# Float32 loads through staging tiles on the hardware DMA queue, q and k by half sequence, reciprocals spread from ScalarE's queue

## The chip, the cores and the metric

The kernel runs on one core of a Trainium2 chip. The metric is the device time of one execution in microseconds (us), as the median of three runs. The engines of the core are named as in the profile: PE (TensorE, with PEld for its weight loads), DVE (VectorE), ACT (ScalarE), POOL (GpSimd) and SP (SyncE, which only issues DMAs here). A name with q behind it (SPq, POOLq) is the sequencer of that engine.

## The reference

Two stages follow each other. First attention over 4 batches, 8 heads, 768 positions and 64 features a head; heads 0, 2 and 6 see all earlier positions, the other five see the first 4 positions (the sinks) and a window of the last 64. Then a feed-forward layer over the 3072 rows, with a gate.

```python
scores = scale * np.matmul(q, k.transpose(0, 1, 3, 2))
stream_keep = causal & (is_sink | in_win)          # heads that are not "retrieval"
scores = np.where(mask[None], scores, -1e9)
a = np.exp(scores - np.max(scores, axis=-1, keepdims=True))
a = a / (np.sum(a, axis=-1, keepdims=True) + 1e-09)
x = np.matmul(a, v)                                # (4, 8, 768, 64) -> (3072, 512)
h = x @ w_in                                       # 512 -> 2048
g = h * (1.0 / (1.0 + np.exp(-beta * h)))
out = g @ w_out                                    # 2048 -> 512
```

All inputs are float32: q, k and v have 6.3 MB each, the two weights 4.2 MB each.

## The kernel before

The work is cut into 8 units: a batch and one half of its 384-query halves (u = 0 or 1). A unit goes through four steps. *pieces_a*: transposes of q and k on PE, scores on PE, their exponential on ACT, masks on DVE, and `sums`, the row sums by PE with a DVE reciprocal `rec`. *pieces_b*: `pv`, the product with v on PE, scaled on DVE into `xT`. *mm1*: 16 steps of four 128x384 matmuls into `h`, each with a tanh on ACT (`t`) and a product on DVE (`gT`). *mm2*: 16 steps of three 128x512 matmuls into `o`, copied by ACT (`osb`) and stored by SP.

The heads go in four pairs. A window head uses a gathered copy of its keys (`KX`, 12 blocks of 128 columns: 4 sinks and 124 positions) and the same of its values (`vs`); the other heads use `KT` and `vr`.

The reciprocals lie one query to a column, with one row to a head, and have to be spread over 64 partitions each. They go through DRAM: three DMAs write `rec` to `rd`, two DMAs read `rd` back 64-fold into `R`. `xT` needs `R`. All five are issued by SP.

All loads are issued by POOL, as DMAs that turn float32 into bfloat16 on the way. q and k come for a whole batch (four DMAs for each pair of heads), v with a POOL copy of the sink rows for each window head. POOL also makes the identity matrix for the transposes and the masks, behind the loads of batch 0 in its program.

The outer loop runs n from 0 to 8. In step n, mm1 of unit n and mm2 of unit n-1 go in 16 steps, and between them the side work: `pv` of unit n+1, then *pieces_a* of unit n+2, so `sums` of unit n+2 is its last piece. Loads of the next batch are issued ahead of a step. Each engine works its instructions off in their order, which a scheduler fixes when the program is built; tiles have a fixed number of buffers in their pool (for example `ps_m` and `ps_h` two, `inp` four).

Of the kernel before, what the change touches and what calls it, by code (L numbers as in the profile page):

```python
# [42 lines left out]
def kernel(  # L43
# [18 lines left out]
    NP = len(PAIRS)  # L62
    W = 64
# [9 lines left out]
    inp = pool("inp", 4)  # L73
    qkp = pool("qkp", 2)
# [14 lines left out]
    def load_pair(b, pi):  # L89
        d = {}  # L90
# [7 lines left out]
        return q2, k2  # L98

    def load_v(b):  # L100
        vr = vp.tile([128, 3, T, D], BF16, name="vr")
        vs = vp.tile([128, 5, NBLK, D], BF16, name="vs")
        sk = vp.tile([SINK, 5, D], BF16, name="sk")
        vpos = {}
        nr = ns = 0
        for pi, pr in enumerate(PAIRS):
            for h in pr:
                if RETR[h]:
                    nc.gpsimd.dma_start(out=vr[:, nr], in_=v[b, h].rearrange("(t p) d -> p t d", p=128))  # L109
                    vpos[h] = nr  # L110
                    nr += 1
                else:
                    vb = v[b, h]
                    nc.gpsimd.dma_start(out=vs[:, ns, 0, :], in_=vb[0:128, :])  # L114
                    nc.gpsimd.dma_start(  # L115
                        out=vs[:, ns, 1:NBLK, :],
                        in_=bass.AP(vb.tensor, vb.offset + (FIRST - W - SINK) * D,
                                    [[D, 128], [STEP * D, NBLK - 1], [1, D]]),
                    )
                    nc.gpsimd.dma_start(out=sk[:, ns, :], in_=vb[0:SINK, :])  # L120
                    nc.gpsimd.tensor_copy(  # L121
                        out=vs[0:SINK, ns, 1:NBLK, :],
                        in_=sk[:, ns, :].unsqueeze(1).to_broadcast([SINK, NBLK - 1, D]),
                    )
                    vpos[h] = ns
                    ns += 1
        return vr, vs, vpos

    qk_in = {}
    v_in = {}  # L130
    for pi in range(NP):
        qk_in[0, pi] = load_pair(0, pi)
    v_in[0] = load_v(0)


# [51 lines left out]
    FS = d_ff // 4  # L187
    for s in range(4):
        for pi, (ha, hb) in enumerate(PAIRS):
            for i, h in enumerate((ha, hb)):  # L190
                nc.gpsimd.dma_start(  # L191
                    out=w_in_sb[i * D:(i + 1) * D, pi, s * FS:(s + 1) * FS],
                    in_=moe_w_in[h * D:(h + 1) * D, s * FS:(s + 1) * FS],
                )
    for s in range(4):
        nc.gpsimd.dma_start(
            out=w_out_sb[:, s * 4:(s + 1) * 4, :],
            in_=moe_w_out[s * 512:(s + 1) * 512, :].rearrange("(fo fi) d -> fi fo d", fi=128),
        )


    qkT = {}

    def transpose_pair(b, pi):
        q2, k2 = qk_in.pop((b, pi))
        ha, hb = PAIRS[pi]
        qt_ps = ps_m.tile([128, T, 128], BF16, name="misc")
        for t in range(T):
            nc.tensor.transpose(qt_ps[:, t, :], q2[:, t, :, :].rearrange("p a d -> p (a d)"), ident)  # L209
        QT = qkp.tile([128, 128, T], BF16, name=f"QT{pi}")  # L210
        nc.vector.tensor_copy(out=QT, in_=qt_ps.rearrange("d t p -> d p t"))
        kt_ps = ps_m.tile([128, T, 128], BF16, name="misc")
        for t in range(T):
            nc.tensor.transpose(kt_ps[:, t, :], k2[:, t, :, :].rearrange("p a d -> p (a d)"), ident)  # L214
        KT = KX = None
        flat = kt_ps.rearrange("d t p -> d (t p)")
        if pi == 0:
            KT = qkp.tile([128, 128, T], BF16, name="KT0")
            nc.vector.tensor_copy(out=KT, in_=kt_ps.rearrange("d t p -> d p t"))
            KT = KT.rearrange("d p t -> d (p t)")  # L220
        else:
            lo = 0
            if pi == 1:
                KT = qkp.tile([128, S], BF16, name="KT1")
                nc.vector.tensor_copy(out=KT[0:64, :], in_=flat[0:64, :])
                lo = 64
            KX = qkp.tile([128, NBLK, 128], BF16, name=f"KX{pi}")
            src = flat[lo:128, :]
            nc.vector.tensor_copy(out=KX[lo:128, 0, :], in_=src[:, 0:128])
            nc.vector.tensor_copy(  # L230
                out=KX[lo:128, 1:NBLK, SINK:128],
                in_=_view(src, FIRST - W, [[STEP, NBLK - 1], [1, 124]]),
            )
# [203 lines left out]
    for f in pieces_l(2):  # L437
        f()
# [50 lines left out]
```

## Time and profile before

| | |
|---|---|
| runs | 312.59, 315.05, 316.58 us, median 315.05 us |
| profiled execution | 314.46 us, its span 312.8 us |
| mean granted clock of TensorE | 0.976 |
| busy | PE 255.1, DVE 147.1, ACT 135.9, POOL 141.7 us |
| DMA moved | 28.66 MB |

Busy time is the union of an engine's instructions; the ends of matmuls are modelled, so a busy PE may still be held up. Instructions that issue DMAs are not busy time in the page's first part. Where one engine waits for another, the profile names the releaser that came last.

### The profile page before, as it was taken

The numbers are of one execution on the slowest core, as the hardware profiler recorded it, in microseconds if no ns is written. First come the engines' busy times: TensorE is split into PE (matmuls) and PEld (weight loads), VectorE is DVE, ScalarE is ACT, GpSimd is POOL, SyncE is SP. The second block draws the span as 40 slices with busy tenths as digits, with TensorE's granted clock in tenths as the row PEclk, the third lists the DMA queues.
The fourth block names the chain that finished last, engine by engine and source line by source line (L and its number), as shares of the span: only waits on it lengthen the run. The fifth ranks groups of instructions, "written<-read, shape, count | busy, mean of one in ns | idle before, by whom it ended". The sixth has DMA issues, their size and how long they took to land.

```text
span 312.8 us, 5541 instructions
## 1 busy us (share of the span) xinstructions
PE 255.1 (82%) x2196; PEld 132.4 (42%) x2196; DVE 147.1 (47%) x309; ACT 135.9 (43%) x217; POOL 141.7 (45%) x208
## 2 busy tenths in 40 slices
PE   0000477659699979999999799999999999999994
PEld 0000353325355433555554345555544455555541
DVE  0000583143489644629773445397736554444410
ACT  1000134513344765534544386355547843455521
POOL 8999899728689967869994100000000000000000
PEclk9999999999979995999999799999999999999999
DMA  9998589999999999989999300500050024000011
GB/s 65 123 102 56 53 108 127 180 217 137 179 80 67 108 202 140 83 134 112 133 111 189 61 34 4 136 34 36 3 135 36 34 67 106 36 35 34 36 67 67
DMA packets 106539, 28.66 MB, mean 92 GB/s; under 512 B 95057, under 2 KB 103441, under 8 KB 106513
## 3 DMA queue, kind: packets, MB, share of 16 engines
q0 software_dynamic: 96256, 15.62, 67.2%
q1 hardware_dynamic: 10256, 12.69, 14.4%
q8 instruction: 17, 0.28, 0.4%
q14 instruction: 10, 0.07, 0.1%
HBM read 37.52 MB, written 6.39 MB: 140 GB/s over the span
## 4 chain that ended last, share of the span: by engine, by line
PE 58%; DMA 21%; POOL 9%; DVE 6%; SPq 2%; issue 2%; ACT 1%; DVEq 0%; POOLq 0%; ACTq 0%
PE o L389 22%; PE h L378 22%; DMA R<-rd 13%; PE sp L291 5%; DMA rd<-rec 4%; PE misc L369 4%; DMA sk<-in_v_dram 3%; PE misc L332 3%; PE misc L214 2%; DVE rec L338 2%; PE misc L209 1%; POOL w_in_sb L191 1%; SPq L345 1%; POOL vs L115 1%; SPq L341 1%
## 5 line engine op out<-in xcount | busy, mean ns | idle before, releaser
L381 ACT ACTIVATE t<-h,beta_h 128x384 f32<-128x384 f32 x128 | 74.3, 582 | 91.0 <-PE h L378 87.9
L378 PE MATMUL h<-xT,w_in_sb 128*128 128x384 bf16 x512 | 110.0, 335 | 0.1
L389 PE MATMUL o<-w_out_sb,gT 128*128 128x512 bf16 x384 | 105.9, 384 | 0.0
L382 DVE SCALAR_TENSOR_TENSOR gT<-t,h 128x384 bf16<-128x384 f32 x128 | 70.4, 552 | 71.4 <-ACT t L381 70.2
L378 PEld LDWEIGHTS <-w_in_sb 128*128 128x128 bf16 x512 | 45.6, 99 | 40.3 <-issue 7.9
L389 PEld LDWEIGHTS <-gT 128*128 128x128 bf16 x384 | 37.0, 98 | 32.6 <-issue 2.4
L209 PE MATMUL misc<-ident,q_99 128*128 128x128 bf16 x6 | 0.8, 303 | 32.6 <-DMA vs<-in_v_dram 32.6
L370 DVE TENSOR_TENSOR xT<-misc,R 128x384 bf16<-128x384 f32 x32 | 16.8, 550 | 13.1 <-DMA R<-rd 10.9
L115 POOL DMA_DIRECT2D vs<-in_v_dram x20 | 21.8, 1092 | 2.1 <-DMA q_642<-in_q_dram 1.7
L121 POOL COPY vs<-sk 4x704 bf16<-4x704 bf16 x20 | 15.2, 762 | 15.7 <-DMA sk<-in_v_dram 8.6
L393 ACT ACTIVATE osb<-o 128x512 f32<-128x512 f32 x24 | 14.3, 594 | 9.1 <-PE o L389 8.6
L293 ACT ACTIVATE es_0_255<-sp 128x768 bf16<-128x768 f32 x2 | 1.6, 811 | 37.9 <-PE sp L291 37.9
L191 POOL DMA_DIRECT2D w_in_sb<-in_moe_w_in_dram x32 | 16.7, 561 | 0.7 <-DMA w_in_sb<-in_moe_w_in_dram 0.7
L369 PEld LDWEIGHTS <-vs 128*64 128x64 bf16 x260 | 9.2, 122 | 15.7 <-issue 15.6
L209 PEld LDWEIGHTS <-q_99 128*128 128x128 bf16 x6 | 0.6, 133 | 32.5 <-issue 32.5
L139 DVE CAST ident<-ident_f 128x128 bf16<-128x128 f32 x1 | 0.2, 227 | 28.2 <-POOL ident_f masks.py:199 28.2
L332 PEld LDWEIGHTS <-esel 128*32 128x32 bf16 x372 | 9.8, 101 | 7.3 <-issue 6.7
L114 POOL DMA_DIRECT2D vs<-in_v_dram x20 | 11.7, 583 | 1.1 <-DMA k_637<-in_k_dram 0.9
L109 POOL DMA_DIRECT2D vr<-in_v_dram x12 | 10.0, 853 | 3.4 <-DMA k_1454<-in_k_dram 2.8
L120 POOL DMA_DIRECT2D sk<-in_v_dram x20 | 10.4, 524 | 0.0
L369 PEld LDWEIGHTS <-vr 128*64 128x64 bf16 x108 | 7.1, 115 | 7.6 <-issue 5.8
L338 DVE RECIPROCAL rec<-misc 96x128 f32<-96x128 f32 x8 | 7.6, 953 | 4.4 <-PE misc L332 4.4
(376 smaller groups left out, 295.8 us busy)
## 6 DMA issues: line engine op xcount, KB each, us to landing
R<-rd SPq DMA_DIRECT2D x16, 384.0 KB
out_dram<-osb SPq DMA_DIRECT2D x24, 256.0 KB
vs<-in_v_dram POOLq DMA_DIRECT2D x20, 176.0 KB, 4.2
w_in_sb<-in_moe_w_in_dram POOLq DMA_DIRECT2D x32, 64.0 KB, 3.7
w_out_sb<-in_moe_w_out_dram POOLq DMA_DIRECT2D x4, 512.0 KB, 12.6
vr<-in_v_dram POOLq DMA_DIRECT2D x12, 96.0 KB, 4.6
rd<-rec SPq DMA_DIRECT2D x24, 4.0 KB
vs<-in_v_dram POOLq DMA_DIRECT2D x20, 16.0 KB, 2.8
```

The lines of the kernel that those rows point to most:

```text
L115: nc.gpsimd.dma_start(out=vs[:, ns, 1:NBLK, :], in_=bass.AP(vb.tensor, vb.offset + (FIRST - W - SINK) * D, [[D, 128], [STEP * D, NBLK - 1] ...
L121: nc.gpsimd.tensor_copy(out=vs[0:SINK, ns, 1:NBLK, :], in_=sk[:, ns, :].unsqueeze(1).to_broadcast([SINK, NBLK - 1, D]),)
L191: nc.gpsimd.dma_start(out=w_in_sb[i * D:(i + 1) * D, pi, s * FS:(s + 1) * FS], in_=moe_w_in[h * D:(h + 1) * D, s * FS:(s + 1) * FS],)
L291: nc.tensor.matmul(o[j][0], o[j][1], o[j][2], start=True, stop=True)
L332: nc.tensor.matmul(sm[32 * j:32 * j + 32, 0:128], esel[:, hpos[h], :, :].rearrange("p a b -> p (a b)"), e, start=(done[j] == 0), stop=(don ...
L369: nc.tensor.matmul(a, l, r, start=st, stop=sp)
L370: nc.vector.tensor_mul(x.xT[:, pi, :], o[:, 0:NQ], x.R[:, pi, :])
L378: nc.tensor.matmul(h[:, 0:NQ], w_in_sb[:, pi, fi * 128:(fi + 1) * 128], x.xT[:, pi, :], start=(pi == 0), stop=(pi == NP - 1))
L381: nc.scalar.activation(out=t, in_=h[:, 0:NQ], func=AF.Tanh, scale=beta_h[:, fi:fi + 1])
L382: nc.vector.scalar_tensor_tensor(out=x.gT[:, fi, :], in0=t, scalar=1.0, in1=h[:, 0:NQ], op0=ADD, op1=MULT)
L389: nc.tensor.matmul(x.o, x.gT[:, fi, ns * 128:(ns + 1) * 128], w_out_sb[:, fi, :], start=(fi == 0), stop=(fi == FO - 1))
L393: nc.scalar.activation(out=osb, in_=x.o, func=AF.Copy, scale=0.5)
```

## The change

All input loads leave POOL. They become float32 DMAs issued by SP into staging tiles, and a cast by an engine follows: k on DVE, q on DVE for batch 0 and on POOL later, v and its sink rows on POOL, the weights on POOL except for two quarters of `w_in` on DVE. q and k are loaded, cast and transposed by half sequence, one DMA for each tensor, pair and half, in runs of 768 bytes; v is loaded by half too, in runs of 256 bytes. Staging tiles have 4 buffers (q, k), 5 (v) or 2 (weights), so a load waits for the cast of the tile that had its buffer. `KX` is kept by half, copied from the transposed keys in SBUF. The order of the outer loop changes: in step n the side work is *pieces_a* of unit n+2 without `sums`, then `pv` of unit n+1, then `sums`; the loads for later units are spread over the 16 steps. The five DMAs that spread the reciprocals are issued by ACT.

```diff
-    inp = pool("inp", 4)
-    qkp = pool("qkp", 2)
+    stg = pool("stg", 2)
+    inp = pool("inp", 2)
+    qkp = pool("qkp", 1)
...
+    def load_pair(b, u, pi):
         ha, hb = PAIRS[pi]
-        q2 = inp.tile([128, T, 2, D], BF16, name="q2")
-        k2 = inp.tile([128, T, 2, D], BF16, name="k2")
-        kfmt = "(p t) d -> p t d" if pi == 0 else "(t p) d -> p t d"
-        for i, h in enumerate((ha, hb)):
-            nc.gpsimd.dma_start(out=q2[:, :, i, :], in_=q[b, h].rearrange("(p t) d -> p t d", t=T))
-            nc.gpsimd.dma_start(out=k2[:, :, i, :], in_=k[b, h].rearrange(kfmt, t=T))
+        for nm, src, eng in (("q2", q, nc.vector if n_first(b, u) else nc.gpsimd), ("k2", k, nc.vector)):
+            f = stg.tile([128, 2, TU, D], F32, name=nm + "f", bufs=4)
+            nc.sync.dma_start(
+                out=f,
+                in_=bass.AP(src.tensor, src.offset + ((b * H + ha) * S + u * NQ) * D,
+                            [[TU * D, 128], [(hb - ha) * S * D, 2], [1, TU * D]]),
+            )
+            c = inp.tile([128, TU, 2, D], BF16, name=nm)
+            cast(eng, c.rearrange("p t a d -> p a t d"), f)
...
+    def load_v(b, h, half):
+        f = stg.tile([128, NBLK // 2, D], F32, name="vf", bufs=5)
...
+        nc.sync.dma_start(
+            out=f[:, w0 - n0:n1 - n0, :],
+            in_=bass.AP(vb.tensor, vb.offset + (FIRST - W - SINK + STEP * (w0 - 1)) * D,
+                        [[D, 128], [STEP * D, n1 - w0], [1, D]]),
+        )
+        cast(nc.gpsimd, vs[:, i, n0:n1, :], f)
+        cast(nc.gpsimd, vs[0:SINK, i, w0:n1, :], sk[:, h, :].unsqueeze(1).to_broadcast([SINK, n1 - w0, D]))
...
+    def load_w_in(s):
+        f = stg.tile([128, 4, FS], F32, name="wf")
...
+        cast(nc.gpsimd if s % 2 else nc.vector, w_in_sb[:, :, r], f)
...
     for s in range(4):
+        load_w_in(s)
+        load_pair(0, 1, s)
+    for h in RH + SH:
+        load_v(0, h, 1)
     for s in range(4):
+        load_w_out(s)
...
         for j in range(3):
-            nc.sync.dma_start(out=rd[:, j, :], in_=rec[32 * j:32 * j + 8, :])
+            nc.scalar.dma_start(out=rd[:, j, :], in_=rec[32 * j:32 * j + 8, :])
...
-            nc.sync.dma_start(
+            nc.scalar.dma_start(
                 out=R[i * D:(i + 1) * D],
...
     for n in range(N + 1):
-        side = pieces_b(n + 1) + pieces_a(n + 2)
-        if n > 0:
-            for f in pieces_l(n + 2):
-                f()
+        lists = [pieces_l(n), pieces_a(n + 2)[:-1] + pieces_b(n + 1) + pieces_a(n + 2)[-1:]]
```

The order of the instructions changes with it. On DVE, around the last reciprocals but one of the main loop, before the change (`rec` belongs to the unit whose `xT` follow; `gT` are steps of mm1):

```order
L338 RECIPROCAL rec<-misc 96x128
L382 SCALAR_TENSOR_TENSOR gT<-t,h 128x384 x6
L370 TENSOR_TENSOR xT<-misc,R 128x384 x2
L382 SCALAR_TENSOR_TENSOR gT<-t,h 128x384
L370 TENSOR_TENSOR xT<-misc,R 128x384 x2
L211 COPY QT_2494<-misc 128x768
```

and the same place now (the `xT` are those of the unit before, L95 is a cast of a staged tile, L252 the copy of transposed q and k):

```order
L409 TENSOR_TENSOR xT<-misc,R 128x384
L338 TENSOR_TENSOR es_1_2443<-es_1_2443,mask_s_201 128x768
L421 SCALAR_TENSOR_TENSOR gT<-t,h 128x384
L409 TENSOR_TENSOR xT<-misc,R 128x384
L421 SCALAR_TENSOR_TENSOR gT<-t,h 128x384
L409 TENSOR_TENSOR xT<-misc,R 128x384
L421 SCALAR_TENSOR_TENSOR gT<-t,h 128x384
L409 TENSOR_TENSOR xT<-misc,R 128x384
L377 RECIPROCAL rec<-misc 96x128
L421 SCALAR_TENSOR_TENSOR gT<-t,h 128x384
L95 CAST k_2230<-k2f 128x2x3x64
L252 COPY QK_2677<-misc 128x2x384
```

What moved: the `xT` of a unit came 6 to 8 steps of mm1 behind its `rec`; now they stand ahead of the next unit's `rec`, about a whole outer step behind their own.

On ACT, at the end of a unit's `sums`, the change puts five DMAs between the tanh of mm1 (`t`), the copies of `o` (`osb`) and the exponentials (`es`):

```order
L420 ACTIVATE t<-h,beta_h 128x384 x5
L380 DMA rd<-rec 8x128 x3
L432 ACTIVATE osb<-o 128x512
L420 ACTIVATE t<-h,beta_h 128x384
L332 ACTIVATE es_1_3153<-sp 128x768
L420 ACTIVATE t<-h,beta_h 128x384
L384 DMA R<-rd 64x4x384 x2
L332 ACTIVATE es_1_3153<-sp 128x768
```

What moved: these DMAs stood on SP, which had little else to do; on ACT four instructions stand between the write of `rd` and the read of it, and those behind each DMA wait with it.

## Rows read from the trace of the kernel before

**Rows 1.** Part 2 of the page: 40 slices, busy tenths, clock, DMA.
```profile
PE   0000477659699979999999799999999999999994
...
POOL 8999899728689967869994100000000000000000
PEclk9999999999979995999999799999999999999999
DMA  9998589999999999989999300500050024000011
```

**Rows 2.** Timeline: start us, us, instruction; first transposes and first matmul of mm1.
```profile
32.03 0.30 POOL masks.py:199 TENSOR_SCALAR_AFFINE_SELECT ident_f<-ident_f 128x128 f32<-128x128 f32 x1
...
32.65 0.80 PE L209 MATMUL misc<-ident,q_99 128*128 128x128 bf16 x6 [32.65 <-DMA vs<-in_v_dram]
...
67.95 0.50 PE L378 MATMUL h<-xT,w_in_sb 128*128 128x384 bf16 x1
```

**Rows 3.** Windows between reciprocals: us, busy by engine, PEclk, DMA share, GB/s.
```profile
69.20:103.20 34.00, 31.02 (x294) 16.72 (x292) 22.68 (x45) 14.26 (x23) 28.11 (x38) 0.95 1.54 117
103.20:129.50 26.30, 24.33 (x225) 11.31 (x224) 13.76 (x29) 16.08 (x27) 21.32 (x28) 0.87 1.54 136
129.50:161.70 32.20, 31.62 (x289) 17.01 (x288) 21.76 (x44) 15.20 (x25) 28.22 (x39) 1.00 1.40 127
161.70:193.00 31.30, 29.36 (x262) 14.20 (x261) 14.23 (x28) 18.30 (x29) 6.76 (x9) 0.95 0.58 77
193.00:224.60 31.60, 31.60 (x289) 16.94 (x290) 21.69 (x44) 15.20 (x25) 0.00 (x0) 1.00 0.18 52
224.60:252.50 27.90, 27.90 (x262) 13.57 (x261) 14.18 (x29) 18.24 (x29) 0.00 (x0) 1.00 0.21 57
```

**Rows 4.** Waits of PE: total us, times, longest us.
```profile
PE misc L369 <- DVE xT L370: 10.7, 5, 3.5
```

**Rows 5.** The chain that ended last: start us, us, what; first reciprocal, later spreads.
```profile
50.47 0.96 DVE rec L338
...
70.79 4.41 DMA rd<-rec
75.83 8.21 DMA R<-rd
...
163.34 2.37 DMA rd<-rec
```

**Rows 6.** Timeline of POOL: last load of q and k of batch 1.
```profile
77.99 0.84 POOL L97 DMA_DIRECT2D k_643<-in_k_dram  x1
```

**Rows 7.** Part 3 of the page: packets, MB, packets' time as share of 16 engines.
```profile
q0 software_dynamic: 96256, 15.62, 67.2%
q1 hardware_dynamic: 10256, 12.69, 14.4%
```

**Rows 8.** One-microsecond windows, columns as in group 3: most loaded, then R alone.
```profile
62.00:63.00 1.00, 0.65 (x22) 0.47 (x15) 0.29 (x1) 0.68 (x1) 0.56 (x1) 1.00 1.15 261
...
199.00:200.00 1.00, 1.00 (x7) 0.51 (x7) 0.00 (x0) 0.24 (x1) 0.00 (x0) 1.00 1.05 200
200.00:201.00 1.00, 1.00 (x7) 0.58 (x6) 0.55 (x1) 0.34 (x1) 0.00 (x0) 1.00 0.89 258
```

**Rows 9.** Tile rd: duration ns min/median/max of the DMA issues on SP.
```profile
L341 SPq DMA_DIRECT2D rd<-rec x24: 268/292/348, 51.4 to 254.1; - x24
L345 SPq DMA_DIRECT2D R<-rd x16: 579/608/1540, 54.7 to 256.1; - x16
```

**Rows 10.** Groups by line: busy us, mean ns of one.
```profile
L381 ACT ACTIVATE t<-h,beta_h 128x384 f32<-128x384 f32 x128 | 74.3, 582 | 91.0 <-PE h L378 87.9 <-DVE QT_784 L211 2.3
```

**Rows 11.** Timeline: a DVE mask product alone, then one beside a POOL copy.
```profile
61.30 0.23 DVE L306 TENSOR_TENSOR es_1_447<-es_1_447,mask_c 128x128 bf16<-128x128 bf16 x1 [3.05 <-ACT es_1_447 L293]
...
124.62 0.76 POOL L121 COPY vs<-sk 4x704 bf16<-4x704 bf16 x1 [1.44 <-DMA sk<-in_v_dram]
...
124.75 0.71 DVE L306 TENSOR_TENSOR es_1_1239<-es_1_1239,mask_c 128x128 bf16<-128x128 bf16 x1 [0.43 <-ACT es_1_1239 L293]
```

More of the change, by code (lines that the diff above doesn't have):

```diff
@@ L62 @@
     NP = len(PAIRS)
+    TU = NQ // 128
     W = 64
@@ L100, in load_v, with cast @@
-    def load_v(b):
+    def cast(eng, dst, src):
+        if eng is nc.scalar:
+            nc.scalar.copy(out=dst, in_=src)
+        else:
+            eng.tensor_copy(out=dst, in_=src)
+    qk_in = {}
+    v_in = {}
+    def load_pair(b, u, pi):
+        ha, hb = PAIRS[pi]
+        res = []
+        for nm, src, eng in (("q2", q, nc.vector if n_first(b, u) else nc.gpsimd), ("k2", k, nc.vector)):
[7 more added lines that the diff above has]
+            cast(eng, c.rearrange("p t a d -> p a t d"), f)
+            res.append(c)
+        qk_in[b, u, pi] = res
@@ L101, in load_v, with n_first, alloc_v @@
+    def n_first(b, u):
+        return b == 0
+    RH = [h for pr in PAIRS for h in pr if RETR[h]]
+    SH = [h for pr in PAIRS for h in pr if not RETR[h]]
+    def alloc_v(b):
         vr = vp.tile([128, 3, T, D], BF16, name="vr")
         vs = vp.tile([128, 5, NBLK, D], BF16, name="vs")
[L103 to L126, printed above, removed]
@@ L136 @@
+    for pi in range(NP):
+        load_pair(0, 0, pi)
+    alloc_v(0)
+    load_sinks(0)
+    for h in RH + SH:
+        load_v(0, h, 0)
     ident_f = consts.tile([128, 128], F32, name="ident_f")
@@ L187 @@
     FS = d_ff // 4
-    for s in range(4):
[L189 to L194, printed above, removed]
+    def load_w_in(s):
+        f = stg.tile([128, 4, FS], F32, name="wf")
+        r = slice(s * FS, (s + 1) * FS)
+        for pi, (ha, hb) in enumerate(PAIRS):
+            if hb == ha + 1:
+                nc.sync.dma_start(out=f[:, pi, :], in_=moe_w_in[ha * D:(ha + 2) * D, r])
+            else:
+                for i, h in enumerate((ha, hb)):
+                    nc.sync.dma_start(out=f[i * D:(i + 1) * D, pi, :], in_=moe_w_in[h * D:(h + 1) * D, r])
+        cast(nc.gpsimd if s % 2 else nc.vector, w_in_sb[:, :, r], f)
@@ L195, with load_w_out @@
+    def load_w_out(s):
+        f = stg.tile([128, 4, FS], F32, name="wf")
+        nc.sync.dma_start(out=f, in_=moe_w_out[s * 512:(s + 1) * 512, :].rearrange("(fo fi) d -> fi fo d", fi=128))
+        cast(nc.gpsimd, w_out_sb[:, s * 4:(s + 1) * 4, :], f)
+    for s in range(4):
+        load_w_in(s)
+        load_pair(0, 1, s)
+    for h in RH + SH:
+        load_v(0, h, 1)
     for s in range(4):
[L196 to L199, printed above, removed]
+        load_w_out(s)
@@ L202 @@
     qkT = {}
[L204 to L229, printed above, removed]
-            nc.vector.tensor_copy(
-                out=KX[lo:128, 1:NBLK, SINK:128],
-                in_=_view(src, FIRST - W, [[STEP, NBLK - 1], [1, 124]]),
-            )
-            nc.vector.tensor_copy(
-                out=KX[lo:128, 1:NBLK, 0:SINK],
-                in_=src[:, 0:SINK].unsqueeze(1).to_broadcast([128 - lo, NBLK - 1, SINK]),
-            )
-        qkT[b, pi] = (QT.rearrange("d p t -> d (p t)"), KT, KX)
@@ L351, in pv @@
     def pv(x, pi):
[L352 removed]
+        vr, vs, vpos, _ = v_in[x.b]
         if pi == 0:
```

102 lines of the change are left out of this document (71 added, 31 removed).

## The prediction, on record before the change was run

> **What bounds the kernel now.** I read the 40 slices first [rows 1]. PE stands idle for the first eighth of the span, while POOL and the DMA engines are full; both stay near full until slice 22 and then fall to nothing, and PE is full from there to the end. So the first half is set by the loads, the second by PE.
>
> Next, where the first half loses time. The first transpose starts at 32.65 us: the identity it needs is made at 32.03 us, behind all of batch 0's loads in POOL's program, and the first matmul of mm1 comes at 67.95 us [rows 2]. Behind it, the windows between reciprocals show how long each outer step takes [rows 3]. The first two lack 3.0 and 2.0 us of PE time, the one that ends at 193.0 lacks 1.9. These holes are PE waiting for `xT`: 10.7 us in 5 waits [rows 4]. `xT` waits for `R`, whose way through DRAM takes 4.41 + 8.21 us where loads are in flight [rows 5]. Behind holes the granted clock falls: windows of mean 0.95, 0.87 and 0.95 [rows 3], the lower of the two levels (1.2 GHz against 2.4) for part of them. The windows of 31.60 and 27.90 us at clock 1.00 have no hole, so they give the price of an outer step that PE fills.
>
> **The change, part by part.** I go from the span, 312.8 us, in four stretches, and add 1.7 us for the profiled execution's own 314.46 us, which stands 0.6 us under the median of 315.05.
>
> *Start to the second reciprocal* (69.2 us before, 1.25 us behind the first mm1). The identity no longer stands behind loads, so what arrives last sets the start. In the changed program the DVE reaches `xT` of unit 0 after the copies of q and k of unit 1, so it needs: q and k of units 0 and 1 (2 x 1.57 MB), the first half of v (1.28 MB), `w_in` (4.19 MB), and one `R` (0.79 MB): 9.4 MB. The rate: `R` alone moved at 200 and 258 GB/s, the most loaded microsecond at 261 [rows 8]; I take 230. That is 41 us, plus 0.8 us of program start and 2.4 us that an almost empty DMA takes to land [rows 5], plus some 4 us for cast, transpose, copies and `pv` (before, four pairs took 17.8 us from the first transpose [rows 2] to the first reciprocal [rows 5], 4.5 a pair): first mm1 at 48, reciprocal at 49.5. Issuing does not set it: 55 DMAs at 0.29 to 0.61 us [rows 9] are 16 to 34 us. **-19.7 us**; from -26 (258 GB/s) to -9 (the 182 GB/s below).
>
> *To the third reciprocal* (34.0 us). PE's own work here is 34.0 less the hole of 3.0 and the clock's 5%, 1.7, so 29.3 us, less some 2.7 since the transposes of the second half move to the next step: 26.5. But it now waits for data. Until q and k of unit 2 are in, the queue carries 9.4 MB plus the second half of v (1.28), `w_out` (4.19), q and k of unit 2 (1.57) and another `R` (0.79): 17.2 MB, 75 us at 230 GB/s. A second way to the same number: a small packet of the software queue took 34.9 ns of an engine and one of the hardware queue 70.3 ns for 1237 bytes [rows 7]; with 9984 runs of 256 bytes at 35 ns, 6144 of 768 bytes at 50, 4096 of 2 KB at 110 and 1024 of 1.5 KB at 85, that is 1.19 ms over 16 engines, 75 us. So the data are there at 78 and the reciprocal at 86, with 4.5 us for the last pair and as much less one for masks and sums, an estimate. In the old kernel the same loads were issued by 78.8 us [rows 6]: the loader itself is not faster by much. 36.5 us, **+2.5**.
>
> *To the fourth* (26.3 us). Less the hole of 2.0 and 13% of clock, 3.4, it is 20.9; the moved transposes add 2: 23. **-3.3**. The loads behind it (unit 3's q and k and batch 1's v, 2.85 MB) need 12 us and are covered by the 23.
>
> *To the eighth* (123.0 us in four steps). The order of DVE puts `xT` a whole step behind its `rec`, so the 13 us of the spread lie beside some 20 us of mm1 and mm2, and the holes go, and with them the clock's dips: 31.6 + 27.8 + 31.6 + 27.9 = 118.9, with 1.1 for the transposes 120. Against it stands **ACT's queue**. A DMA on ACT holds the tanh behind it until `rec` is there, and that of `R` until `rd` has landed. From `rd` to `R` pass 2.4 us quiet, 4.4 loaded [rows 5]; between them stand four instructions, at 0.58 us or more each [rows 10], so 2.3 us are filled. Issuing costs 3 x 0.29 + 2 x 0.61 = 2.1 us of ACT's sequencer a unit [rows 9]. ACT itself is busy 15 to 18 us of 28 to 32 [rows 3], and two buffers of `h` let PE run about two steps ahead. Lower bound 0; upper 4.4 + 1.0 for `rec` + 2.1 - 2.3 = 5.2 us a unit, 31 in six. I take 0.7 us a unit, 4 in all, near the lower end, since the quiet landing is the nearer row and the buffers cover the rest. The casts go beside idle time: DVE has 14 to 22 us of work in a step, POOL none late [rows 3]. With the port below, 1 us more: 125. **+2.0**.
>
> *Tail* (from 252.5 us to the end, 60.3 us): the order of both programs has the same matmuls left behind the last `sums`, and no loads. **0**.
>
> Sum: -19.7 + 2.5 - 3.3 + 2.0 = -18.5; 312.8 - 18.5 + 1.7 = **296 us**.
>
> **A rule against the change.** POOL now casts beside DVE. A mask product on DVE took 0.23 us alone, but 0.71 beside a POOL copy of 0.76 us that began 0.13 us ahead of it; it ended when the copy did [rows 11]. A unit has some 17 POOL casts, about 6 us of its 30 if they go at the copy's 1.1 ns an element, and about 12 DVE instructions that could meet them: a fifth of them, held 0.2 us each, is 0.5 us a unit, on an engine that is half idle. That gives the 1 us above; if all met, 12 x 0.5 x 8 = 48 us of DVE time, which still fits its idle half.
>
> The Trainium skill (SBUF — State Buffer, section "SBUF: two separate sides") says that VectorE and GpSimd take turns at a shared port pair, for a whole instruction, where the VectorE operation has two SBUF inputs or runs in a two-port mode. The row of 0.71 us agrees with it. By that rule the casts on GpSimd could lengthen the DVE's part of the chain, which would raise the sum by a few us and make no case of its own.
>
> **Rivals.**
>
> 1. *Slower: the hardware queue is poor at short runs.* Almost everything that it carried before had 1.5 or 2 KB; now q and k come in 768 and v in 256 bytes. If each short packet took 70.3 ns like a long one, the stream to unit 2 would take 104 us in place of 75: 296 + 29 = 325 us; a step's loads would then take 36 us of DMA against PE's 30, and four steps more would make it 348. It decides from 182 GB/s downward, where the stream takes 94 us and the gain is gone. For it: no row shows short loads on this queue. Against it: the software queue's short packets took half as long. 10%.
> 2. *ACT waits.* If the landing under load holds ACT, 3 to 5 us a unit, the main loop gives back 14 to 27 more: 310 to 323. For it: SP waited for `rd` in every unit before, and loads now run all along. Against it: four instructions and two `h` buffers of cover. 12%.
> 3. *The loader was the bound and stays it.* The same bytes in the same order, a staging tile that waits for its cast, or DVE held in its order by a cast whose load is late, and the third reciprocal comes at 100 rather than 86: 310, the gain of the order alone. For it: POOL had issued the same loads by 78.8 us. Against it: PE needed 24 us from there to its reciprocal, with holes that go. 10%.
> 4. *More gain.* At 258 GB/s or better the third reciprocal is PE's to set, at 75 to 78, and ACT loses nothing: 280 to 285. 12%.
>
> My forecast has the remaining 56%, with 287 to 306 as its own range.
>
> **How the numbers follow.** Time 296 us. The range of 8 in 10 takes in the fourth rival and the lower half of the second and third: 281 to 316. About 2% is what this measurement can tell from no change: under 308.7 us counts as faster, over 321.4 as slower. Faster: 0.54 from the forecast, 0.12 from the fourth, 0.04 from the edges of the second and third, 0.70. Slower: 0.08 from the first, 0.04 from the second, 0.12. Same: the rest, 0.18.
>
> **What would show it.** Right: first transposes before 10 us, first mm1 at 44 to 53, third reciprocal at 80 to 92, no wait of PE for `xT` in the main loop, clock 1.00 in the windows from the fourth reciprocal on, 27 to 33 us to a step. Wrong: PE waits for `t` or `h` behind the DMAs of ACT (rival 2); moved bytes under 180 GB/s in the first 80 us with SP waiting for staging tiles or the queue (rivals 1, 3); holes ahead of the transposes of later units, which would say that the prefetch of one step is too short.

## The result, and the profile after

The changed kernel takes 299.76 us (median of 4 runs, 298.76 to 301.12); the kernel before took 313.82 us beside it (310.78 to 316.58). The ratio of the two is 0.959, with a 95% interval of 0.949 to 0.968: faster by 4%. The forecast was 296 us with a range of 281 to 316. The profiled execution has a span of 299.4 us, 13.4 us under the 312.8 of before. (Here and below a median takes in every run of a kernel and a ratio only those within 1.5% of its fastest, and since the profiled executions of experiments 1 and 9 are not among those, the stretches of 9 are left out and what 1 lost late is told as that execution's alone.)

The windows between reciprocals, with the columns of [rows 3]: the first row goes from the first to the second reciprocal, the last from the eighth to the end.

```profile
23.31:58.08 34.77, 14.43 (x154) 7.62 (x154) 17.13 (x27) 8.11 (x10) 9.77 (x15) 1.00 0.94 218
58.08:92.94 34.86, 27.64 (x256) 14.51 (x259) 23.84 (x54) 12.99 (x21) 13.65 (x16) 0.95 0.86 247
92.94:117.67 24.73, 23.13 (x250) 12.01 (x253) 19.57 (x40) 15.55 (x26) 11.78 (x26) 1.00 0.83 199
117.67:148.43 30.76, 30.48 (x265) 15.96 (x269) 22.14 (x57) 16.08 (x28) 14.39 (x33) 1.00 0.80 193
...
239.08:299.40 60.32, 56.20 (x325) 28.47 (x331) 21.15 (x38) 24.72 (x43) 0.00 (x0) 1.00 0.17 58
```

Against [rows 3] the start up to the second reciprocal is 11.1 us shorter (58.1 for 69.2), the next stretch 0.9 longer, the third 1.6 shorter, the four steps to the eighth reciprocal 1.6 shorter (121.4 for 123.0), and the tail the same. The clock is 0.95 in the stretch to the third reciprocal and stands at 1.00 in the steps, where before it had dipped.

The waits of PE, in the columns of [rows 4]. The holes for `xT`, 10.7 us in [rows 4], are down to 1.3 us (the last line). Beside the start itself, the longest left are waits for q and k, the last of them, for `k_737` of unit 2, at 76 us.

```profile
PE misc L248 <- DVE ident L165: 6.9, 1, 6.9
PE misc L248 <- DVE q_250 L95: 5.7, 1, 5.7
...
PE misc L248 <- DVE k_737 L95: 3.8, 1, 3.8
...
PE misc L248 <- DVE k_254 L95: 2.4, 1, 2.4
PE misc L248 <- DVE q_234 L95: 2.4, 1, 2.4
...
PE misc L408 <- DVE xT L409: 1.3, 2, 0.6
```

Why q and k come late is told by the chain that ended last (start, us, what). From 28 to 75 us it is nearly all DMA, and each transfer hangs on an earlier transfer that has nothing to do with its data, or on the cast that empties a staging tile: the load of `w_in` is issued when `R` has landed, the load of k of unit 2 (`k_737`) behind `w_out`.

```profile
23.31 0.96 DVE rec L377
25.19 1.95 DMA rd<-rec
28.02 10.30 DMA R<-rd
38.81 5.67 DMA wf<-in_moe_w_in_dram
44.50 3.55 DMA vf<-in_v_dram
48.05 1.88 POOL w_in_sb L95
50.25 2.69 DMA vf<-in_v_dram
52.96 8.52 DMA wf<-in_moe_w_out_dram
61.53 1.90 POOL w_out_sb L95
63.87 10.91 DMA k2f<-in_k_dram
74.80 1.54 DVE k_737 L95
```

The reason stands in the program itself, and the trace has it too, as the semaphore that each DMA waits for and the one that it counts up. A DMA of SP or ScalarE signals its end on one of eight counters, taken in turn by both, and waits until the last user of its counter has landed. Here, in program order, are the spread of unit 0 on ScalarE, which takes counters 0, 1, 3 and 7 among others, and the loads of SP that come upon it:

```
ScalarE  L380 rd<-rec   waits for counter 0 and the reciprocal
         L380 rd<-rec   waits for counter 1
         L380 rd<-rec   waits for counter 3
         L384 R<-rd     waits for counters 0, 1, 3 and 7
SP       L223 w_in      waits for counter 6
         L220 w_in      waits for counter 0
         L105 q         waits for counter 1 and its staging tile
         ...
         L220 w_in      waits for counter 6
         L223 w_in      waits for counter 7
```

So a load of SP can wait for an `rd`, which waits for its reciprocal, or for an `R`. SP's waits up to 60 us (total, times, longest) show it:

```profile
SPq L228 <- DMA rd<-rec: 7.1, 1, 7.1
SPq L223 <- DMA R<-rd: 4.8, 1, 4.8
SPq L220 <- DMA rd<-rec: 2.7, 1, 2.7
```

and SP's timeline (start, us, instruction) has the stretches in which nothing is issued, 24.1 to 26.8 us ahead of the load that waits for counter 0, and 30.3 to 35.1 ahead of the one that waits for counter 7:

```profile
22.40 1.67 SPq L223 DMA_DIRECT2D wf<-in_moe_w_in_dram  x2
26.76 0.35 SPq L220 DMA_DIRECT2D wf<-in_moe_w_in_dram  x1
...
29.71 0.58 SPq L220 DMA_DIRECT2D wf<-in_moe_w_in_dram  x1
35.12 1.11 SPq L223 DMA_DIRECT2D wf<-in_moe_w_in_dram  x2
```

Last, the queues, as in [rows 7]:

```profile
q1 hardware_dynamic: 68896, 37.54, 48.1%
```

48.1% of 16 engines over 299.4 us, divided by 68896 packets, is 33.4 ns a packet of 545 bytes in the mean. By size, the packets of this queue took 19.6 ns for 256 bytes, 43.6 for 768 and 105.2 for 2048, where the prediction took 35, 50 and 110. Short runs on the hardware queue cost no more than on the software queue in [rows 7].

### The profile page after: what moved, and what is told of

It reads as the page before. It is cut to its first block, busy times and chain, and to the rows that moved or that the text cites. A ratio compares the mean times of both kernels' runs of the same rounds, so it can differ in the third digit from the quotient of the medians.

```text
span 299.4 us, 5780 instructions
## 1 busy us (share of the span) xinstructions
PE 248.5 (83%) x2167; PEld 130.2 (43%) x2196; DVE 178.8 (60%) x407; ACT 133.0 (44%) x217; POOL 74.1 (25%) x150
## 3 DMA queue, kind: packets, MB, share of 16 engines
q1 hardware_dynamic: 68896, 37.54, 48.1%
## 4 chain that ended last, share of the span: by engine, by line
PE 51%; DMA 21%; DVE 14%; SPq 4%; ACT 4%; issue 3%; POOL 2%; ACTq 1%; DVEq 0%
PE h L417 21%; PE o L428 19%; DMA R<-rd 6%; DMA k2f<-in_k_dram 5%; DMA vf<-in_v_dram 5%; PE sp L330 4%; DMA wf<-in_moe_w_out_dram 3%; PE misc L408 3%; PE misc L371 2%; DVE gT L421 2%; DMA wf<-in_moe_w_in_dram 2%; PE misc L248 2%; SPq L105 2%; SPq L146 1%; ACT t L420 1%
## 5 line engine op out<-in xcount | busy, mean ns | idle before, releaser
L417 PE MATMUL h<-xT,w_in_sb 128*128 128x384 bf16 x512 | 106.5, 330 | 2.9 <-DVE gT L421 2.3
L420 ACT ACTIVATE t<-h,beta_h 128x384 f32<-128x384 f32 x128 | 73.0, 581 | 74.4 <-PE h L417 70.1
L428 PE MATMUL o<-w_out_sb,gT 128*128 128x512 bf16 x355 | 96.2, 379 | 1.8 <-issue 0.6
L95 POOL CAST vs<-vf 128x384 bf16<-128x384 f32 x40 | 21.3, 533 | 14.3 <-DMA vf<-in_v_dram 14.0
L95 POOL CAST vs<-sk 4x320 bf16<-4x320 f32 (+1 forms) x40 | 19.6, 490 | 2.5
L95 POOL CAST vr<-vf 128x192 bf16<-128x192 f32 x24 | 8.2, 359 | 30.3 <-DMA vf<-in_v_dram 30.0
L332 ACT ACTIVATE es_1_496<-sp 128x768 bf16<-128x768 f32 x5 | 4.1, 811 | 16.4 <-PE sp L330 16.4
L95 POOL CAST w_in_sb<-wf 128x2048 bf16<-128x2048 f32 x2 | 3.8, 1894 | 30.0 <-DMA wf<-in_moe_w_in_dram 15.5
L95 POOL CAST w_out_sb<-wf 128x2048 bf16<-128x2048 f32 x4 | 7.6, 1895 | 11.7 <-DMA wf<-in_moe_w_out_dram 11.7
L330 PE MATMUL sp<-QK_336 64*128 64x384 bf16 (+2 forms) x18 | 3.5, 429 | 7.1 <-DVE QK_336 L252 4.4
L332 ACT ACTIVATE es_0_338<-sp 128x768 bf16<-128x768 f32 x2 | 1.6, 811 | 11.2 <-PE sp L330 11.2
L332 ACT ACTIVATE es_1_1212<-sp 128x768 bf16<-128x768 f32 x5 | 4.0, 809 | 5.3 <-PE sp L330 4.6
```

The lines of the kernel that those rows point to most:

```text
L95: eng.tensor_copy(out=dst, in_=src)
L330: nc.tensor.matmul(o[j][0], o[j][1], o[j][2], start=True, stop=True)
L332: nc.scalar.activation(out=es[:, ri, 0:nh, :], in_=sp[:, 0:nh, 0:NQ], func=AF.Exp, scale=scale)
L417: nc.tensor.matmul(h[:, 0:NQ], w_in_sb[:, pi, fi * 128:(fi + 1) * 128], x.xT[:, pi, :], start=(pi == 0), stop=(pi == NP - 1))
L420: nc.scalar.activation(out=t, in_=h[:, 0:NQ], func=AF.Tanh, scale=beta_h[:, fi:fi + 1])
L428: nc.tensor.matmul(x.o, x.gT[:, fi, ns * 128:(ns + 1) * 128], w_out_sb[:, fi, :], start=(fi == 0), stop=(fi == FO - 1))
```

## The experiments

Each kernel is the changed one with one edit, unless it says otherwise. They ran in four groups, each on a chip of its own: 1 to 4, 5 to 8, 9 to 11, and 12. The kernel before took 312.7, 314.1, 310.2 and 311.0 us there (medians; single runs from 306 to 317). Times of one group compare directly; between groups a difference of 4 us is not told apart by them alone, and the ratio to the kernel before says more. For group 5 to 8 the ratio rests on one run of the kernel before, 307.6 us (the seven lie between 307.6 and 317.4); it has no interval and says little. A table at the end of this section has the reciprocals.

**1. The spread on POOL's queue.**

```diff
-            nc.scalar.dma_start(out=rd[:, j, :], ...
+            nc.gpsimd.dma_start(out=rd[:, j, :], ...
-            nc.scalar.dma_start(out=R[...], ...
+            nc.gpsimd.dma_start(out=R[...], ...
```

> The five DMAs of each reciprocal's spread (rd and R) move from ScalarE's hardware queue to POOL's software queue; all else as in the changed kernel (299.8 us). Theory (the loads of SP and the spread of ScalarE go round the same eight completion semaphores, so a load waits until the DMA eight issues before it has landed, be it an rd that waits for its reciprocal): SP's waits for rd and R in the first 65 us go (they are 20 us and more there), the second reciprocal comes at 52 to 55 us instead of 58.1, the third at 86 to 90 instead of 92.9, the steps behind stay at 121 us, total 291 to 296. Rival (ScalarE loses time behind the spread): the two first reciprocals stay within 1 us, the four steps to the eighth get 3 us or more shorter. Rival (POOL pays in its place): POOL holds its casts of v and w behind an rd that waits for its reciprocal, the third reciprocal comes later than 93 us, total 300 to 308.

302.7 us (297.5 to 303.7; ratio 0.964, 0.948 to 0.980). The second reciprocal came at 52.7, the third at 88.7, both as the theory said, and SP's waits for `rd` and `R` before 58 us are gone. The total did not come. The fourth reciprocal is back at 117.9, since POOL issues `R` of unit 2 only between its casts, 10 us behind the reciprocal. The chain of this kernel:

```profile
88.71 0.04 DVE rec L377
...
98.62 9.49 DMA R<-rd
...
108.23 0.56 DVE xT L409
```

That much is this execution's; the other runs lie between 297.5 and 303.6 us.

**2. The spread on SP's queue**, with the same edit to `nc.sync`.

> The five DMAs of the spread go back to SP's queue, where the kernel before had them; loads, staging and order stay as in the changed kernel. Theory (a load must not stand behind the spread): now SP itself stops at each rd until the reciprocal is there, with all later loads behind it, so the second reciprocal comes 3 to 10 us later than 58.1, the third later than 96 us, total 303 to 315. Rival (the place of the spread is worth nothing, the loads and their staging alone set the start): all reciprocals within 1.5 us of the changed kernel, 298 to 302 us.

304.4 us (303.6 to 306.1; ratio 0.980, 0.972 to 0.988). The total is as the theory said, its course is not: the second reciprocal comes at 51.7, earlier than on ScalarE, but the first mm1 only at 67.0 (57.2), and the loss is one wait of PE for `xT` of 12.9 us, since `R` stood behind loads in SP's program. The four steps to the eighth reciprocal take 121.7 us, as with the spread on ScalarE (121.4), so ScalarE had lost nothing by carrying it.

```profile
PE misc L408 <- DVE xT L409: 12.9, 1, 12.9
```

**3. The old order in the changed kernel.**

```diff
-        lists = [pieces_l(n), pieces_a(n + 2)[:-1] + pieces_b(n + 1) + pieces_a(n + 2)[-1:]]
+        lists = [pieces_l(n), pieces_b(n + 1) + pieces_a(n + 2)]
```

> The changed kernel with the side order of the kernel before: pv of unit n+1 ahead of transposes and scores of unit n+2, instead of between those and the last sums. Theory (the new order covers the spread and gave the gain of the steps): PE waits for xT again, 8 us or more in all instead of 1.3, the granted clock falls to 0.85 to 0.95 in some steps, the time from the second to the eighth reciprocal is 184 to 190 us instead of 181.0, total 303 to 309. Rival (with prefetched halves the spread lands in time in any order): within 1.5 us of 299.8. The first reciprocals stay where they are by both.

315.3 us (313.3 to 315.9; ratio 1.013, 1.003 to 1.023): worse than expected by both, and no faster than the kernel before. The second reciprocal is 15 us earlier than before, and 3.9 earlier than in the changed kernel, where both cases had it stay; the fourth at 129.6 stands where it stood (129.5). PE waits for `xT` for 17.5 us, and the clock is 0.87 and 0.90 in the two windows in which the start's gain is lost:

```profile
PE misc L408 <- DVE xT L409: 17.5, 5, 7.9
```

```profile
54.16:94.52 40.36, 29.96 (x268) 15.30 (x272) 23.88 (x59) 14.08 (x23) 15.93 (x22) 0.87 0.74 212
94.52:129.64 35.12, 31.20 (x281) 16.42 (x283) 20.33 (x41) 18.41 (x30) 11.90 (x26) 0.90 0.71 176
```

**4. The new order in the kernel before.**

```diff
-        side = pieces_b(n + 1) + pieces_a(n + 2)
+        side = pieces_a(n + 2)[:-1] + pieces_b(n + 1) + pieces_a(n + 2)[-1:]
```

> The kernel before with the side order of the changed kernel alone (loads on POOL's software queue, whole sequences, spread on SP). Theory (order and loads are separate gains): the first reciprocals stay at 50.5 and 69.2 us, PE's waits for xT fall from 10.7 to under 3 us, the stretch from the second to the eighth reciprocal falls from 183.3 us by 3 to 6, total 307 to 312 against 313.8. Rival (the transposes of a whole sequence, now ahead of pv, cost what the order gains): 313 to 318. Rival (order is the whole gain and the loads gave nothing): 300 us.

302.9 us (302.2 to 303.3, and one run of 438.4; ratio 0.974, 0.966 to 0.982), a larger gain than any case but the last gave it. PE's waits for `xT` are 2.3 us in all, the steps to the eighth reciprocal take 118.4 us, less than in the changed kernel (121.4). The order alone thus gives 12.1 of the 13.4 us of span.

**5. `w_out` behind q and k of unit 2.**

```diff
     for h in RH + SH:
         load_v(0, h, 1)
-    for s in range(4):
-        load_w_out(s)
 ...
     for f in pieces_a(0) + pieces_a(1) + pieces_b(0) + pieces_l(-1):
         f()
+    for s in range(4):
+        load_w_out(s)
```

> The changed kernel with the four loads of w_out issued behind q and k of unit 2 instead of ahead of them; nothing else. Theory (between the second and the third reciprocal PE waits for k of unit 2, which stands behind w_out and behind the spread of unit 1 in SP's program; in the changed kernel it is cast at 74.8 us): the k cast comes at 60 to 66 us, PE's wait of 3.8 us for it goes, the third reciprocal comes 3 to 7 us earlier than 92.9, mm2 waits at most 3 us for w_out, total 293 to 297. Rival (the same bytes in another order: what k gains, w_out loses, and mm2 waits in its place): third reciprocal within 1.5 us of 92.9, total 298 to 302. The second reciprocal stays at 58 by both.

298.3 us (296.6 to 299.5; 0.970 of before): the total is the rival's, the course the theory's. The first k cast of unit 2 comes at 58.7 us, PE's wait for it goes, and the third reciprocal comes 9.9 us earlier, more than expected. The fourth, at 113.3, keeps 4.4 of that, since mm2 work that was done before the third reciprocal (6.4 us of PE's time in the changed kernel, none here) now stands behind it. That the second comes at 54.7 instead of 58.1 was expected by neither case. The loads up to the last k of unit 1 are those of the changed kernel, here as in experiment 3, and still these two come 3.4 and 3.9 us earlier; with one profiled execution of each, why stays open.

**6. `w_in` in 6 transfers.**

```diff
-    def load_w_in(s):        # columns s of all pairs: 6 DMAs, 24 in all
+    def load_w_in(pi):       # whole rows of one pair: 1 or 2 DMAs, 6 in all
+            nc.sync.dma_start(out=g, in_=moe_w_in[ha * D:(ha + 2) * D, :])
```

> The changed kernel with w_in loaded by pair of heads in 6 transfers of whole 8 KB rows instead of 24 of 2 KB rows; the same bytes, staging tiles and casts. Theory (at most eight transfers of SP and ScalarE are under way, and each load waits for the one eight before it: with 18 transfers fewer, more bytes are under way and the spread of unit 0 holds up fewer loads): SP's idle stretches before 40 us shrink from 9.8 us to under 5, the second reciprocal comes at 50 to 54 us instead of 58.1, the third at 87 to 91, total 292 to 298. Rival (the bytes set the start, at some 200 GB/s whatever their form): second reciprocal within 1.5 us of 58.1. Rival (a wait is only moved: the first matmul of mm1 now needs all of w_in): second reciprocal at 60 us or later.

296.4 us (294.5 to 297.5; 0.964 of before), second reciprocal 51.4, third 86.5: the numbers of the theory, but not its reason. SP stands idle longer, not shorter (4.7, 3.8 and 7.3 us before 40 us). The queue still moved more in the first 40 us, 219 GB/s for 190 (the last number; first the changed kernel, then this one):

```profile
0.00:40.00 40.00, 11.47 (x116) 7.00 (x117) 20.65 (x71) 8.26 (x10) 10.17 (x30) 1.00 0.82 190
```

```profile
0.00:40.00 40.00, 14.63 (x137) 8.47 (x138) 24.22 (x78) 11.49 (x14) 10.20 (x30) 1.00 0.89 219
```

That the same eight transfers, being larger, have more bytes under way while SP stands idle would explain it, but is not shown.

**7. Both.** Edits of 5 and 6.

> w_out behind q and k of unit 2 and w_in in 6 transfers, together, on the changed kernel. If the two limits are apart from each other (the spread's hold on the loads before the second reciprocal, the order of loads before the third), the gains add: second reciprocal at 50 to 54, third at 80 to 86, fourth at 105 to 111, total 286 to 293. If the stream of bytes is the one limit of the first 95 us, third reciprocal at 89 or later and total above 296.

293.9 us (293.0 to 296.8; 0.955 of before): second reciprocal 51.8, third 80.4, fourth 109.8. The reciprocals lie where they were expected, but the gains add only in part: the second comes 6.3 us before the changed kernel's where the edits alone gave 3.4 and 6.7, the third 12.6 where they gave 9.9 and 6.4. The total lies just above the expected 286 to 293.

**8. Both, and the spread of units 0 and 1 on POOL.**

```diff
+        q_eng = nc.gpsimd if x.b == 0 else nc.scalar
-            nc.scalar.dma_start(out=rd[:, j, :], ...
+            q_eng.dma_start(out=rd[:, j, :], ...
```

> As the kernel before it in this list (w_out later, w_in in 6 transfers), and the spread of units 0 and 1 alone on POOL's queue, the others on ScalarE's. Theory (the spread of the first two units holds the loads, and only there; later POOL's queue delays the spread behind casts): second reciprocal 1 to 3 us earlier than with both alone, steps from the fourth reciprocal on as in the changed kernel (121 us), total 284 to 291. Rival (POOL held by an rd delays the casts of w_in and v by as much): second reciprocal the same or later than with both alone.

298.1 us (297.8 to 298.6; 0.969 of before), 4 us worse than both alone: the second reciprocal is 0.5 us earlier, the third 3.9 later. POOL, held by `rd`, casts late, and SP then waits for staging tiles (6.6 us for a cast of `w_in`, 7.0 for one of q). The loads' coupling to the spread had only changed its engine, much as the rival said.

**9. One cast for q and k.**

```diff
-            c = inp.tile([128, TU, 2, D], BF16, name=nm)
-            cast(eng, c.rearrange("p t a d -> p a t d"), f)
+        c = inp.tile([128, TU, 2, 2, D], BF16, name="qk")
+        cast(eng, c.rearrange("p t x a d -> p (x a) t d"), f.rearrange("p x a t d -> p (x a) t d"))
```

> The changed kernel with q and k of a pair of heads staged in one tile and cast by one instruction (DVE and POOL in turn by pair, DVE alone in batch 0), so that the six transposes of a pair and a half stand in one row on PE. Theory (the steps behind the fourth reciprocal are 3.0 us longer than with the old loads in the same order, 121.4 against 118.4, because 96 transposes in rows of three keep PE busy for 10.6 us where rows of six took 8.0): their busy time falls to 7.5 to 8.5 us and the four steps to 118 to 120, total 295 to 299. Rival (the steps are longer since PE waits for DVE, which has 82.7 us of work there instead of 73.6): transposes get cheaper but the four steps stay within 0.7 us of 121.4. Rival (the fused cast needs both loads, and the first reciprocals come later): second reciprocal 1 to 3 us later, total 299 to 302.

296.5 us (293.8 to 299.5; ratio 0.956, 0.950 to 0.962), the ratio of the changed kernel. The transposes of the four steps got no cheaper: with the same cast they keep PE busy for 9.83 us in experiment 10. Both figures of the expectation, 10.6 and 8.0 us, were misreadings, sums of groups that overlap; by windows they took 9.14 in the changed kernel and 6.67 with the old loads:

```profile
117.67:239.08 121.41, 9.14 (x96) 1.00 0.51 124
```

```profile
121.96:240.39 118.43, 6.67 (x96) 1.00 0.67 84
```

So the transposes keep PE busy for 2.5 us more than with the old loads, of the 3.0 by which the steps are longer than in experiment 4. But this does not settle the steps' length: in experiment 10 the steps take 119.8 us, with the dearest transposes of the three. Why the transposes are dearer, and what makes the steps longer, stays open.

**10. All three.** Edits of 5, 6 and 9.

> w_out behind q and k of unit 2, w_in in 6 transfers (293.9 us with these two) and the fused cast, together. If the rows of transposes cost 2.6 us in the steps behind the fourth reciprocal and some more ahead of it: 289 to 292. If the fused cast only moves a wait: 293 to 297.

295.6 us (293.6 to 301.9; ratio 0.954, 0.949 to 0.958): the fused cast gives nothing in the total that these runs can tell (the four steps take 119.8 us, 121.1 in experiment 7), and 293.9 without it (on another chip) is no slower.

**11. The kernel before, with the new order and the constants first.** The edit of 4, and the identity and masks moved in the program text:

```diff
+    ident_f = consts.tile([128, 128], F32, name="ident_f")
+    make_identity(nc, ident_f)
+    ...
     for pi in range(NP):
         qk_in[0, pi] = load_pair(0, pi)
     v_in[0] = load_v(0)
-    ident_f = consts.tile([128, 128], F32, name="ident_f")
-    make_identity(nc, ident_f)
-    ...
```

> The kernel before with the side order of the changed kernel (302.9 us) and, besides, the identity and the masks built ahead of the loads in POOL's program; the loads stay on POOL's software queue, whole sequences. Theory (the start of the transposes is worth little by itself, since the stream of loads to w_in, w_out and the next q and k sets when the second and third steps can go): first transposes at 10 to 14 us instead of 32, first reciprocal at 28 to 38 instead of 50.2, second at 58 to 64 instead of 67.7, third at 93 to 97 instead of 97.1, total 299 to 302. Rival (what stood behind the loads was the whole start): all reciprocals come 10 us earlier or more, total 289 to 293. Rival (nothing to gain): second reciprocal within 1.5 us of 67.7, 302 to 304.

292.0 us (291.3 to 292.9; ratio 0.945, 0.941 to 0.949): the lowest median of all, 3.6 us under experiment 10 on the same chip; 7, on another, is not told from it. The theory was wrong, and its rival right in the total; of the reciprocals the third came only 4.2 us before experiment 4's, not 10. With the old loads, still on the software queue, the first transposes start at 7.8 us, the second reciprocal comes at 41.5, and mm1 starts at 40.3, while `w_in` is still being loaded:

```profile
7.76 0.80 PE L209 MATMUL misc<-ident,q 128*128 128x128 bf16 x6 [7.76 <-DMA q<-in_q_dram]
...
40.32 0.82 PE L378 MATMUL h<-xT,w_in_sb 128*128 128x384 bf16 x2
```

Its third reciprocal, at 92.9, is where the changed kernel has it, but PE has by then done far more (62.7 us of work for 50.2). The first 60 us show it, of this kernel, of the changed one and of the kernel of experiment 12:

```profile
0.00:60.00 60.00, 38.06 (x320) 19.65 (x321) 25.98 (x71) 20.80 (x29) 51.95 (x91) 1.00 1.14 111
```

```profile
0.00:60.00 60.00, 24.51 (x276) 14.18 (x276) 33.02 (x91) 13.94 (x17) 19.90 (x45) 1.00 0.89 216
```

```profile
0.00:60.00 60.00, 32.16 (x308) 17.96 (x309) 34.01 (x100) 18.45 (x26) 18.33 (x45) 1.00 0.89 206
```

The first number behind the comma is PE's busy time: 38.1, 24.5 and 32.2 us.

**12. q and k of unit 1 ahead of `w_in`.**

```diff
     for s in range(4):
+        load_pair(0, 1, s)
+    for s in range(4):
         load_w_in(s)
-        load_pair(0, 1, s)
```

> The changed kernel with q and k of unit 1 (the second half of batch 0) loaded ahead of w_in instead of between its four slices; the same transfers, queues, staging and side order. Theory (PE's program has all scores of unit 1 ahead of the first mm1, so with its last q and k behind the last slice of w_in no matmul of mm1 can run beside the loads of w_in; the old loads, with constants ahead, had all q and k in first and ran mm1 on the first slices from 40.3 us): second reciprocal at 38 to 46 us instead of 58.1, first mm1 at 40 to 47 instead of 57.2, PE busy for 30 to 38 us of the first 60 instead of 24.5, total 288 to 295. Rival (the spread's hold on SP's loads is the limit): PE's busy time in the first 60 us stays under 27 us, total 297 to 300. Rival (what is won here is lost at the k of unit 2 and at w_out, as before): second reciprocal early, third at 91 to 94, total 295 to 299.

296.5 us (295.2 to 298.1; ratio 0.955, 0.951 to 0.960). The first mm1 comes at 42.2 instead of 57.2 and PE's busy time in the first 60 us is 32.2, as the theory said. The second reciprocal, at 49.8, is later than it said, and the total is the third case's: k of unit 2 is still behind `w_out`, and the third reciprocal, at 88.6, keeps 4.3 us. By its ratio the whole is not told from the changed kernel.

The reciprocals and the spans of the profiled executions, in us, with PE's busy time in the first 60 us:

```
                                  2nd    3rd    4th    8th    span   PE, 0 to 60
before                           69.2  103.2  129.5  252.5   312.8   18.4
4  before, new order             67.7   97.1  122.0  240.4   300.7   18.7
11 the same, constants first     41.5   92.9  113.1  229.7   289.9   38.1
changed                          58.1   92.9  117.7  239.1   299.4   24.5
3  changed, old order            54.2   94.5  129.6  253.2   313.5   27.4
1  spread on POOL                52.7   88.7  117.9  241.1   301.9   26.9
2  spread on SP                  51.7   92.6  120.2  241.9   301.8   21.7
5  w_out later                   54.7   83.1  113.3  234.6   294.9   25.7
6  w_in in 6                     51.4   86.5  112.3  234.0   294.6   27.8
7  5 and 6                       51.8   80.4  109.8  230.9   291.3   27.5
8  the same, 2 spreads on POOL   51.3   84.3  114.0  235.9   296.6   30.0
10 5, 6 and the fused cast       52.3   81.0  112.8  232.5   292.9   28.4
12 unit 1 ahead of w_in          49.8   88.6  114.9  234.3   294.6   32.2
```

## Why the prediction was right in time, and where it failed

**The time.** 299.8 us came for 296, in the forecast's own range of 287 to 306. That it lies so near is in part luck. The first of the five terms missed by 8.6 us. The others came out 3.5 us better than forecast, which covers part of it: +0.9 for +2.5 to the third reciprocal, -1.6 for -3.3 to the fourth, -1.6 for +2.0 to the eighth, and 0 for the tail. To the third the difference is near, but both of its ends came late, by 8.6 and 6.9 us. To the eighth the sign is the other one, since 3.6 of the 5 us that were put aside for ScalarE's queue and for casts beside DVE did not come. And the span, 299.4 us, is 5.1 over the 294.3 forecast; the median is only 3.8 off because the profiled execution was the slowest of the four. Two of the signs named for a right forecast missed: the first mm1 (44 to 53) came at 57.2 and the third reciprocal (80 to 92) at 92.9.

**The start, the failed term.** -19.7 was forecast and -11.1 measured: the first mm1 came at 57.2, not 48. The step took the start to be a stream of 9.4 MB at 230 GB/s, with issue left out as 16 to 34 us of work. It did not ask what each load waits for: in the first 40 us the queue moved 190 GB/s (experiment 6 has the line), and the last k of unit 1 had landed at 49.2 us where 44.2 was forecast (41 + 0.8 + 2.4). From there to the first mm1 took 8.0 us in place of some 4. So some 5 us of the miss are the stream's and some 4 belong to the work behind it, in which POOL's cast of `w_in` held a DVE mask product for 1.96 us (rows in the last section).

Two things show in the runs: SP's loads wait for the spread (the second reciprocal comes 5.4 and 6.4 us earlier without that wait in experiments 1 and 2, and 6.7 with fewer transfers in 6), and q and k of unit 1 stand between slices of `w_in` (experiment 12: 8.3 us, and mm1 15 us earlier). They overlap, and do not add. And experiments 3 and 5 keep both and still come 3.4 to 3.9 us before the changed kernel; against these two, only 1.5 to 3.3 us are left for experiments 1, 2 and 6, and 4.4 to 4.9 for 12. How the 8.6 us divide is therefore not settled.

**The order and the loads.** The prediction's terms hold a split that it never drew. Holes and clock were priced at 3.0 + 1.7, 2.0 + 3.4 and 4.1 us, 14.2 in all; the order alone gave 12.1 of span (experiment 4). The other 4.3 of the 18.5 us were the net worth of all the rest, and measured on top of the order that gives 1.3 of span and 3.1 between medians of two chips, with ratios whose intervals overlap. So the gain of this change is the order's, but for a rest that these runs do not tell from nothing; experiment 3 says the same from the other side. The third rival called 310 us "the gain of the order alone"; that price was wrong by 7 us, mostly because it kept the four steps at 125 us, where the order alone needs 118.4; the third reciprocal, put at 100, comes at 97.

**What the start's gain needed.** The prediction rightly saw that the identity stood behind the loads, but tied its release to the new loads. Experiment 11 unties them: order and constants alone give a ratio of 0.945 (0.941 to 0.949), the whole change 0.959 (0.949 to 0.968). On one chip it is 292.0 against 296.5 us for experiment 9, whose ratio is that of the changed kernel. So the new loads as a whole (queue, staging, halves and the place of the spread) cost some 4 us here where a gain was forecast. With another order and fewer transfers the cost is smaller at most: experiment 10 is 3.6 us behind on the same chip, 7 on another is not told from 11, and no run has the new loads ahead. How the cost divides between the shared counters, the order of loads and the casts is not settled.

**To the third reciprocal.** Data were forecast at 78 and the reciprocal 8 us later, at 86. The last k of unit 2 was cast at 79.8, but the reciprocal came at 92.9, 13 us behind: DVE (the third busy time) works for 9.2 of the 10 us from 80 to 90, with casts, copies and masks in one queue:

```profile
80.00:90.00 10.00, 8.50 (x97) 4.24 (x96) 9.23 (x30) 4.26 (x6) 3.52 (x7) 0.95 0.84 210
```

The work behind the last load was priced too low, not the stream, which moved 227 GB/s up to 80 us (230 in the forecast).

**The rivals.** Short runs are not slow (33.4 ns a packet), so the slower rival fell. ScalarE's DMAs cost PE nothing that shows: in the four steps its longest waits, 0.6 us in all, are for DVE, and without these DMAs the steps were no shorter (experiment 2). The wait that the rival put on ScalarE sat on SP instead, through the shared counters. The fourth rival wanted the third reciprocal at 75 to 78; not even experiment 7 reached that.

```profile
PE h L417 <- DVE gT L421: 0.6, 3, 0.2
```

## What to carry to other kernels

Ask of every load what it waits for besides its buffer: here a load on one hardware queue waited for a transfer on another, and so for compute. Change the order and the place of the constants before the loads: those two edits beat the whole rewrite of the loads (the constants without the order were not run). And compare kernels by PE's work done at a time, not by one event: two had the third reciprocal at 92.9 us and ended 9.5 us apart.

## What the runs showed of the hardware

A POOL cast can hold a DVE instruction until it ends, but does not hold each one. In the changed kernel a mask product of 128x128, 0.23 us alone [rows 11], took 1.96 beside POOL's cast of `w_in`, while an `xT`, which reads PE's result `misc`, kept its 0.56 beside a cast of `w_out`. First DVE's rows, then POOL's:

```profile
48.05 1.96 DVE L345 TENSOR_TENSOR es_1_532<-es_1_532,mask_c 128x128 bf16<-128x128 bf16 x1 [1.74 <-ACT es_1_532 L332]
...
58.99 0.56 DVE L409 TENSOR_TENSOR xT<-misc,R 128x384 bf16<-128x384 f32 x1
```

```profile
48.04 1.89 POOL L95 CAST w_in_sb<-wf 128x2048 bf16<-128x2048 f32 x1 [14.53 <-DMA vf<-in_v_dram]
...
58.14 1.90 POOL L95 CAST w_out_sb<-wf 128x2048 bf16<-128x2048 f32 x1 [1.74 <-DMA wf<-in_moe_w_out_dram]
```

The cast of `k_737` in the chain above, 1.54 us for 0.35 alone, ended just behind a cast of `w_out` (74.23 to 76.13 us). A row of POOL casts can hold for all of theirs. In experiment 8, DVE's cast of k, 0.35 us alone, took 4.11. POOL was in a cast of q when it began, and two casts of `w_out` followed, 3.73 us together. First DVE's rows, then POOL's:

```profile
59.83 0.35 DVE L95 CAST k<-k2f 128x384 bf16<-128x384 f32 x1
...
61.97 4.11 DVE L95 CAST k<-k2f 128x384 bf16<-128x384 f32 x1
```

```profile
61.23 0.96 POOL L95 CAST q<-q2f 128x384 bf16<-128x384 f32 x2
62.13 3.73 POOL L95 CAST w_out_sb<-wf 128x2048 bf16<-128x2048 f32 x2
```

The prediction had priced a hold at 0.2 to 0.5 us, from a copy of 0.76 us [rows 11]; here it was up to 3.8 us, on DVE's way to the third reciprocal.

The Trainium skill (SBUF — State Buffer, section "SBUF: two separate sides") calls the shared port pair an exclusive lock between a GpSimd operation and a DVE operation in a two-port mode or with two inputs in SBUF: whoever starts first keeps it for the whole instruction. The 1.96 and 4.11 us agree, and so do the 0.56. That the waiting engine does not get its turn between two instructions of the other is shown by the 4.11 us alone; in the changed kernel a cast of k at 51.32 us, beside a row of shorter POOL casts, took 0.66.
